# Putting the transfer queue of a top-k attention and feed-forward kernel into the program's order

## The chip, the core and the metric

The kernel runs on one core of a Trainium2 chip. Its engines are TensorE (PE, with weight loads shown apart as PEld), VectorE (DVE), ScalarE (ACT), GpSimd (POOL) and SyncE (SP). All transfers of this kernel are issued by SP, one after the other; "SPq" is that queue in the profile. The metric is the device time of one execution in microseconds, lower is better; shown is the median of the runs.

## What is computed

Inputs are q, k and v of 8 batches, 8 heads, 576 positions and 64 values per head, all float32, and two weight matrices of 512 x 2048 and 2048 x 512.

```python
scores = scale * np.matmul(q, k.transpose(0, 1, 3, 2))
kth = np.partition(scores, -top_k, axis=-1)[..., -top_k:-top_k + 1]      # top_k = 32
scores = np.where(scores >= kth, scores, -1000000000.0)
attn = np.exp(scores - np.max(scores, axis=-1, keepdims=True))
attn = attn / (np.sum(attn, axis=-1, keepdims=True) + 1e-09)
x = np.matmul(attn, v)            # then the heads side by side: (4608, 512)
h = x @ w_in
g = np.where(h >= 1, h, np.where(h <= -1, 0.0, (h + 1) ** 2 / 4.0))
out = g @ w_out
```

## The kernel before

**Steps.** A batch has four row tiles of 128 positions (t = 0 to 3) and a tail of 64 (t = 4). A step m treats two rows tiles of scores, 128 x 576 each: a pair of heads of a whole tile, or four heads of a tail. There are 144 steps; `steps` (line 606) lists them in rounds of two batches: b's four tiles (16 steps), b's tail (2), b+1's tail (2), b+1's four tiles (16).

**What a step does.** PE multiplies queries and keys (`sp`, L358), ACT copies the scores out (`s`, L359). DVE finds the 32nd largest of each row by repeated max and match-replace (L379 to L451) and masks the exponentials (L458); its reciprocal of the sums (`rz`, L404) opens the next step. POOL scales the weights `e` by it (L411). The weights are then needed with positions on partitions. In the first 8 steps and the last 2 PE transposes them (`transpose_w`). In the other 134 steps `move_w` (L484) does it through memory: ACT splits each 32-bit word into two 16-bit halves (`halves`, L488, one buffer), SP writes them out (`rows<-halves`, L490), waits until they have landed, and issues a transposing read (`wT<-rows`, L492; four `wT` buffers). PE multiplies `wT` by the values (`po`, L506, or L514 for tails), always for a pair of steps, in an even step: those of m-4 and m-3. The odd one of the pair is thus the one whose weights are fresher.

**Second layer.** Once all heads of 128 positions are there, `mlp` queues their matrix products (`ph`, L539, and `py`, L578). PE takes them in small portions spread over the following steps; the result `y` (L581) goes out at L583.

**Keys, queries and values of later batches.** From batch 2 on, keys and queries are turned in the same way as the weights. `turn` (L279) has ACT split a block into `parts` (L283, one buffer), writes `lines<-parts` (L285), and keeps the transposing read (`kT<-lines` or `qT<-lines`, L292) for `finish_turns`. `turned_keys_of` (L294) goes through five blocks of a batch's keys, one in every second step, each loaded by two or three transfers (`k_block`, L303 to L307) into one buffer. Its first call also starts `load_values` (L190): four loads of `v_in` (two buffers, so the batch before last must be done), two of `v_tail` for whole tiles and four for tails (L198, L203). `queries` (L706) turns the queries of a coming tile and fetches the next one's (`q_in`, L211, one buffer).

**Early part.** Before the second layer can start, its weights are converted in 32 pieces (`convert`, L632) in the first 8 steps; their words are loaded into `raw` and into the parts of `kT` and `v_in` that aren't used yet (L134). Later, every second step, half a piece is loaded again and inspected (L169).

**Order.** `tc.manual_schedule` (L680) fixes the order of PE, DVE, ACT and POOL to that of the program. SP isn't in that list: the order of its transfers was chosen by the scheduler, which moves a transfer to a place where its inputs and buffer are expected to be free. The program's main loop (L766) runs seven slots for each step; `move_w` is called in slot 3, and calls `finish_turns` itself.

Of the kernel before, what the change touches and what calls it, by code (L numbers as in the profile page):

```python
# [11 lines left out]
F32 = mybir.dt.float32  # L12
U16 = mybir.dt.uint16
# [13 lines left out]
def kernel(  # L27
# [10 lines left out]
    nc = tc.nc  # L38
    B, H, S, D = q.shape
    NTOK, DM = out.shape  # L40
    DFF = moe_w_in.shape[1]
    P = 128
# [3 lines left out]
    NHP = H // 2  # L46
# [34 lines left out]

    v_tails = []
    for i in range(2):
        v_tails.append([const.tile([P, H, D], F32, name=f"v_tail{i}{x}") for x in range(2)])
        for x in v_tails[i]:
            nc.gpsimd.memset(x, 0.0)

# [89 lines left out]
    def run(ctx, paired):  # L177
# [12 lines left out]
        def load_values(b):  # L190
            v_in = stage.tile([P, H, NT, D], F32, name="v_in")
            v_tl = v_tails[b % 2]
            yield v_in, v_tl
            for h in range(0, H, 2):
                nc.sync.dma_start(out=v_in[:, h:h + 2], in_=whole(v, b)[:, h:h + 2])
                yield
            for j in range(2):
                nc.sync.dma_start(out=v_tl[0][j * TL:(j + 1) * TL, j::2, :],  # L198
                                  in_=v[b, j::2, SM:S, :].rearrange("h p d -> p h d"))
            yield  # L200
            for hp in range(NHP):
                g = hp % 2
                nc.sync.dma_start(out=v_tl[1][g * TL:(g + 1) * TL, 2 * hp:2 * hp + 2, :],  # L203
                                  in_=v[b, 2 * hp:2 * hp + 2, SM:S, :].rearrange("h p d -> p h d"))
                if g:
                    yield

        def load_queries(b, t):
            if t < NT:
# [75 lines left out]
            nc.sync.dma_start(out=lines, in_=parts)  # L285
            turns.append(partial(nc.sync.dma_start_transpose, dst.bitcast(U16), lines.rearrange("p t k -> (p t) k")))

        turns = []

        def finish_turns():  # L290
            while turns:
                turns.pop(0)()  # L292

        def turned_keys_of(b):  # L294

            kT = stage.tile([P, NHP, S], F32, name="kT")
            got = dict(kT=kT)

            def load_block(c):
                x = stage.tile([P, H, D], F32, name="k_block", tag="k_in", bufs=1)  # L300
                ends = k[b, :, SM:S, :].rearrange("h p d -> p h d")
                if c < NT:
                    nc.sync.dma_start(out=x[:, 0::2, :], in_=whole(k, b)[:, 0::2, c, :])  # L303
                    nc.sync.dma_start(out=x[TL:P, 1::2, :], in_=whole(k, b)[0:P - TL, 1::2, c, :])
                else:
                    nc.sync.dma_start(out=x[0:TL, 0::2, :], in_=ends[:, 0::2, :])
                nc.sync.dma_start(out=x[0:TL, 1::2, :], in_=whole(k, b)[P - TL:P, 1::2, c - 1, :] if c else ends[:, 1::2, :])  # L307
                return x

            blocks = {0: load_block(0)}  # L310
            got["loads"] = load_values(b)
            got["v"], got["v_tl"] = next(got["loads"])
            yield got
            for c in range(NT + 1):
                n = P if c < NT else TL
                turn(blocks.pop(c)[0:n], kT[:, :, c * P:c * P + n])
                if c < NT:
                    blocks[c + 1] = load_block(c + 1)
                yield got

        def turned_queries_of(q_in, t):
# [162 lines left out]
        def move_w(st):  # L484
            st["wT"] = wT = late.tile([P, BLOCKS, P], F32, name="wT", bufs=4)
            halves = late.tile([P, 2, 2 * S], U16, name="halves")
            for i in range(2):
                nc.scalar.copy(halves[:, :, i * S:(i + 1) * S], st["e"][:, i, :].bitcast(U16).rearrange("p (k t) -> p t k", t=2))  # L488
            rows = dram.tile([P, 2, 2 * S], U16, name="rows")
            nc.sync.dma_start(out=rows, in_=halves)  # L490
            finish_turns()
            nc.sync.dma_start_transpose(wT.bitcast(U16), rows.rearrange("p t k -> (p t) k"))  # L492

        def block(i, c):
            return i * (NT + 1) + c if c < NT else NT
# [2 lines left out]
        def values(st):  # L498
            t, hp, v_in, v_tl = st["t"], st["hp"], st["keys"]["v"], st["keys"]["v_tl"]
            wT = st["wT"]  # L500
            po = ps.tile([P, P], F32, name="po", tag="ph", bufs=3)
            if t < NT:
                for c in range(NT + 1):
                    for j in range(2):
                        h = 2 * hp + j
                        nc.tensor.matmul(po[j * D:(j + 1) * D], v_in[:, h, c, :] if c < NT else v_tl[0][:, h, :],  # L506
                                         wT[:, block(j, c)], start=(c == 0), stop=(c == NT))
            else:
                for i in range(2):
                    cols = slice(i * TL, (i + 1) * TL)  # L510
                    for c in range(NT + 1):
                        for j in range(2):
                            h = 2 * (hp + i) + j
                            nc.tensor.matmul(po[j * D:(j + 1) * D, cols], v_in[:, h, c, :] if c < NT else v_tl[1][:, h, :],  # L514
                                             wT[:, block(i, c), part(i, j)],
                                             start=(c == 0), stop=(c == NT))
            xT, col = st["xT"]
            if t < NT:
                nc.scalar.copy(xT[:, hp, col:col + P], po)
            else:  # L520
                nc.scalar.copy(xT[:, hp:hp + 2, col:col + TL], po.rearrange("p (i n) -> p i n", i=2))
# [149 lines left out]
        def advance(amount, until):  # L671
# [4 lines left out]
            while pending and due >= pending[0][0] and pe_time < until and take():  # L676
# [1 line left out]
            due = min(due, 24.0)  # L678

        order = tc.manual_schedule(engines={mybir.EngineType.PE, mybir.EngineType.DVE, mybir.EngineType.Activation,  # L680
                                            mybir.EngineType.Pool})
        order.__enter__()
        keys, xTs = {}, {}
        q_ins, qTs = {}, {}
# [1 line left out]
        def fetch(i):  # L686
            if i < len(rounds) and rounds[i] not in q_ins:
                q_ins[rounds[i]] = load_queries(*rounds[i])
# [17 lines left out]
        def queries(m):  # L706
            nonlocal pe_time
            if m < n and steps[m][0:2] not in qTs:
                r = steps[m][0:2]
                if r[0] > 1:  # L710
                    qTs[r] = turned_queries_of(q_ins[r], r[1])
                else:
                    qTs[r] = queries_of(q_ins[r], r[1], nc.vector.tensor_copy if m == 0 else nc.scalar.copy)
                    pe_time += 0.5
                fetch(rounds.index(r) + 1)

        def begin(m):
            b, t, hp, ch, col = steps[m]
# [20 lines left out]
        for i in range(2, len(room) or 2):  # L739
            load(words, i)  # L740
        queries(0)
        convert(12.0)
        begin_at(0)
        convert(13.0)
# [21 lines left out]
        for m in range(n + 2):  # L766
# [22 lines left out]
            for slot in range(SLOTS):  # L789
                now = start + (dve_time - start) * (slot + 1) / SLOTS  # L790
                for _ in range(parts[slot]):
                    next(top_k, None)
                if m < n and converted < n_pieces:
                    if slot in now_converting:
                        convert(now)
                elif slot == 3 and late is not None:
                    if m % 2:
                        inspect()
                    elif paired:
                        load(late, inspected, 1, 2)  # L800
                if slot == 1 and 1 <= m <= n and state[m - 1]["by_tensor"]:
                    pe_time = max(pe_time, done[m - 1] + 2.0) + 1.0
                    transpose_w(state[m - 1])
# [1 line left out]
                if slot == 3 and 1 <= m <= n and state[m - 1] is not None and not state[m - 1]["by_tensor"]:  # L805
                    move_w(state[m - 1])
                    ready_at[m - 1] = done[m - 1] + 15.0
                if slot == 3:
                    finish_turns()
                if slot == 2 and m == n and paired:  # L810
                    judge(ps, att)
                if slot == 2 and (early or m == first_late or m >= n - 1):
                    values_until(m)
# [14 lines left out]
                if slot == (6 if early else 1):  # L828
                    queries(m + (3 if early else 5))
                    if (m < n and prep is None and next_keys < B and steps[m][0] == next_keys - 1 and steps[m][1] >= 1  # L830
                            and (next_keys > 1 or converted == n_pieces)):
                        prep = (turned_keys_of if next_keys > 1 else keys_of)(next_keys)
                    if prep is not None and (m % 2 == 0 or next_keys == 1):
                        got = next(prep, None)
                        pe_time += 0.5 if next_keys < 2 else 0.0
                        if got is None:
                            prep, next_keys = None, next_keys + 1
                        else:
                            keys[next_keys] = got
                            value_loads = got.get("loads", value_loads)  # L840
                    elif value_loads is not None:
                        next(value_loads, None)
                if paired and early and spent == 0 and not pending:
                    rest = ps.tile([P, NT, P], F32, name="rest", tag="py", bufs=1)
                    for i in range(5):
# [59 lines left out]
```

## Time and profile before

| | |
|---|---|
| time, median of 3 runs | 1481.04 us (1479.47 to 1487.06) |
| profiled execution | 1484.11 us |
| its span | 1482.2 us |
| busy: PE, DVE | 1435.8, 1403.9 us |
| busy: ACT, POOL | 1158.0, 926.6 us |
| DMA queue | 510144 packets, 258.80 MB, 66.4% of 16 engines |
| writes `rows<-halves` | 134, 576 KB each |
| transposing reads `wT<-rows` | 134, about 2.6 us of SP each, 4.7 us from issue to landing |
| loads `v_tail<-in_v_dram` | 16 of 64 KB and 32 of 32 KB |
| granted PE clock, mean | 0.992 |

Busy times are unions of the intervals in which an engine works; they come from the one profiled execution. A line of a timeline gives start and duration in us, engine, source line, operation, written tile and what it is made from, the count of merged instructions, and in brackets the idle time before it and what ended that. A line of waits gives the waiting engine and line, what released it, the total in us, the number of times, and the longest. A line of the chain of waits gives start, duration and the work on the chain that ended last. Where an instruction waited for several things, the release names the one that came last in the records, which may not be the one that counted.

### The profile page before, as it was taken

How to read it: one execution, taken by the hardware profiler on the slowest of the kernel's cores; microseconds unless marked ns; L12 is line 12 of the kernel's file. 1: busy time of each engine (PE TensorE's matmuls, PEld its weight loads, DVE VectorE, ACT ScalarE, POOL GpSimd, SP SyncE). 2: the span in 40 equal slices, each digit the busy share in tenths (PEclk: the TensorE clock that was granted, in tenths of full speed). 3: DMA queues.
4: the chain of work that ended last, by engine and by line, in shares of the span. 5: the costliest groups of instructions: out<-in, count | busy, mean ns of one | idle time of the engine just before them, and what ended most of it. 6: DMA issues, size and time to landing. Idle time of an engine off the chain costs nothing.

```text
span 1482.2 us, 32086 instructions
## 1 busy us (share of the span) xinstructions
PE 1435.8 (97%) x10755; PEld 1044.6 (70%) x10755; DVE 1403.9 (95%) x4392; ACT 1158.0 (78%) x2221; POOL 926.6 (63%) x1310
## 2 busy tenths in 40 slices
PE   6998899999999999999999999999999999999998
PEld 5766677777777777767777777677777777777675
DVE  6989999999999999999999999999999999999912
ACT  7987877878888887887778888788778888777632
POOL 3474566776676666566766677567666666666730
PEclk8999999999999999999999999999999999999999
DMA  8633657775677767787677787787677886665510
GB/s 252 196 121 107 177 152 203 196 194 162 167 206 204 193 193 205 193 209 174 163 195 203 196 198 194 195 214 183 174 197 187 202 202 167 168 166 142 149 25 17
DMA packets 510319, 260.94 MB, mean 176 GB/s; under 512 B 460992, under 2 KB 469184, under 8 KB 510144
## 3 DMA queue, kind: packets, MB, share of 16 engines
q1 hardware_dynamic: 510144, 258.80, 66.4%
q8 instruction: 87, 1.43, 0.4%
q14 instruction: 88, 0.72, 0.2%
HBM read 62.91 MB, written 102.63 MB: 112 GB/s over the span
## 4 chain that ended last, share of the span: by engine, by line
PE 80%; DVE 10%; DMA 4%; ACT 4%; issue 2%; SPq 1%; ACTq 0%; DVEq 0%
PE ph L539 30%; PE py L578 29%; PE sp L358 9%; PE po L506 9%; DVE more L379 2%; DMA rows<-halves 2%; DVE e L458 2%; DMA wT<-rows 1%; PE po L514 1%; DVE more L372 1%; DVE tops L420 1%; DVE tops L428 1%; DVE tops L392 1%; PE pw L473 1%; ACT halves L488 1%
## 5 line engine op out<-in xcount | busy, mean ns | idle before, releaser
L539 PEld LDWEIGHTS ph<-xT,w_in 128*128 128x128 f32 x4608 | 547.0, 192 | 102.6 <-issue 71.1
L539 PE MATMUL ph<-xT,w_in 128*128 128x128 f32 x4608 | 555.7, 276 | 2.3 <-ACT g L558 1.4
L578 PE MATMUL py<-w_out,g 128*128 128x512 f32 x1152 | 541.5, 597 | 1.8 <-ACT y L581 1.8
L565 POOL TENSOR_SCALAR r<-r 128x256 f32<-128x256 f32 x280 | 166.9, 596 | 413.4 <-ACT r L550 409.7
L379 DVE MATCH_REPLACE8 more<-tops,more 128x288 f32<-128x288 f32 x864 | 375.1, 437 | 0.0
L578 PEld LDWEIGHTS py<-w_out,g 128*128 128x128 f32 x1152 | 199.0, 191 | 166.5 <-issue 163.8
L488 ACT COPY halves<-e 128x1152 uint16<-128x1152 uint16 x268 | 293.6, 1143 | 18.5 <-DMA rows<-halves 18.1
L568 POOL TENSOR_TENSOR g<-r,g 128x256 f32<-128x256 f32 x280 | 241.6, 863 | 22.0
L458 DVE SCALAR_TENSOR_TENSOR e<-s,kth,e 128x577 f32<-128x577 f32 x288 | 246.9, 893 | 0.1
L411 POOL TENSOR_SCALAR e<-e,rz 128x576 f32<-128x576 f32 x268 | 235.9, 890 | 13.2 <-DVE rz L404 13.2
L395 ACT ACTIVATE e<-s,nmax 128x576 f32<-128x576 f32 x288 | 222.5, 773 | 4.7
L550 ACT ACTIVATE r<-ph,half 128x256 f32<-128x256 f32 (+1 forms) x296 | 136.1, 460 | 107.8 <-PE ph L539 99.7
L359 ACT ACTIVATE s<-sp 128x576 f32<-128x576 f32 x288 | 171.9, 649 | 61.7 <-PE sp L358 57.7
L567 POOL TENSOR_TENSOR r<-r 128x256 f32<-128x256 f32 x276 | 183.1, 663 | 23.0
L358 PE MATMUL sp<-kT,qT 64*128 64x288 f32 x1024 | 163.1, 436 | 8.3 <-ACT kT L261 6.1
L506 PE MATMUL po<-wT,v_in 128*64 128x128 f32 x2048 | 138.8, 277 | 8.0 <-DMA wT<-rows 4.6
L358 PEld LDWEIGHTS sp<-kT,qT 64*128 64x128 f32 x1024 | 90.0, 189 | 79.3 <-issue 37.2
L506 PEld LDWEIGHTS po<-wT,v_in 128*64 128x64 f32 x2048 | 113.6, 137 | 32.4 <-issue 10.3
L558 ACT ACTIVATE g<-ph,minus 128x256 f32<-128x256 f32 x280 | 130.4, 466 | 0.0
L372 DVE TENSOR_TENSOR more<-s 128x576 f32<-128x576 f32 x144 | 124.1, 862 | 6.0 <-ACT s L359 6.0
L420 DVE MAX8 tops<-more 128x8 f32<-128x288 f32 x288 | 125.4, 443 | 0.0
L372 DVE TENSOR_TENSOR less<-s 128x576 f32<-128x576 f32 x144 | 117.7, 817 | 0.0
(91 smaller groups left out, 1370.0 us busy)
## 6 DMA issues: line engine op xcount, KB each, us to landing
rows<-halves SPq DMA_DIRECT2D x134, 576.0 KB, 3.3
lines<-parts SPq DMA_DIRECT2D x48, 256.0 KB, 3.1
q_in<-in_q_dram SPq DMA_DIRECT2D x32, 256.0 KB, 3.8
v_in<-in_v_dram SPq DMA_DIRECT2D x32, 256.0 KB, 4.5
out_dram<-y SPq DMA_DIRECT2D x32, 256.0 KB, 3.9
raw<-in_moe_w_in_dram SPq DMA_DIRECT2D x32, 256.0 KB, 3.3
raw<-in_moe_w_out_dram SPq DMA_DIRECT2D x32, 256.0 KB, 3.5
kT<-in_moe_w_in_dram SPq DMA_DIRECT2D x8, 512.0 KB, 5.2
```

The source lines that it names most:

```text
L358: nc.tensor.matmul(*x, start=True, stop=True)
L372: nc.vector.tensor_tensor(out=x, in0=s[:, :, 0:SH], in1=s[:, :, SH:S], op=op)
L379: nc.vector.match_replace(out=st["rest"][:, i, :], in_to_replace=eight(st["tops"], i, r - 8), in_values=src[:, i, :], imm_value=LOWEST)
L395: nc.scalar.activation(e[:, i, :], s[:, i, :], AF.Exp, bias=nmax[:, i:i + 1])
L411: nc.gpsimd.tensor_scalar(st["e"][:, i, :], st["e"][:, i, :], rz[:, i:i + 1], 1.0, ALU.mult, ALU.mult)
L458: nc.vector.scalar_tensor_tensor(out=st["all"][1][:, i, :], in0=st["all"][0][:, i, :], scalar=last[i], in1=st["all"][1][:, i, :], op0=ALU. ...
L488: nc.scalar.copy(halves[:, :, i * S:(i + 1) * S], st["e"][:, i, :].bitcast(U16).rearrange("p (k t) -> p t k", t=2))
L506: nc.tensor.matmul(po[j * D:(j + 1) * D], v_in[:, h, c, :] if c < NT else v_tl[0][:, h, :], wT[:, block(j, c)], start=(c == 0), stop=(c == ...
L539: nc.tensor.matmul(ph[:, i], w_in[:, kk, f * P:(f + 1) * P], xT[:, kk], start=(kk == 0), stop=(kk == NK - 1))
L567: nc.gpsimd.tensor_tensor(out=r, in0=r, in1=r, op=ALU.mult)
L568: nc.gpsimd.tensor_tensor(out=g, in0=r, in1=g, op=ALU.add)
L578: nc.tensor.matmul(py[0], gs[f // group][:, f % group], w_out[:, f, :], start=(f == 0), stop=(f == NF - 1))
```

## The change

SP joins the engines that keep the program's order, and the program now says in which order its transfers go. `turns` still holds reads of lines; two more lists hold the reads of rows and the loads, and `issue` empties a list. A step issues the reads of rows of the step before in slot 0; lines where `turn` is called (slot 1); the load for inspection in slot 1 instead of slot 3; rows in slot 3, then the reads of lines, then the loads of keys, queries and values, which were only noted when they came up. In the last three steps and after, a read of rows may go in any slot.

The loads of tails get fewer: a tail step's values now come from two places. Heads whose half of the partitions is right in the first tile (`v_tl[0]`) are taken from there; the second tile (`v_tl[1]`) is half as large and holds the other four heads, with two transfers instead of four. The check of the inspection (`judge`) moves from slot 2 of step n to the end of step n+1.

```diff
-        v_tails.append([const.tile([P, H, D], F32, name=f"v_tail{i}{x}") for x in range(2)])
+        v_tails.append([const.tile([P, H // (x + 1), D], F32, name=f"v_tail{i}{x}") for x in range(2)])
...
             yield
-            for hp in range(NHP):
-                g = hp % 2
-                nc.sync.dma_start(out=v_tl[1][g * TL:(g + 1) * TL, 2 * hp:2 * hp + 2, :],
-                                  in_=v[b, 2 * hp:2 * hp + 2, SM:S, :].rearrange("h p d -> p h d"))
-                if g:
-                    yield
+            for x in range(2):
+                nc.sync.dma_start(out=v_tl[1][x * TL:(x + 1) * TL, x::2, :],
+                                  in_=v[b, x + 1::4, SM:S, :].rearrange("h p d -> p h d"))
+            yield
+
+        def tail_values(v_tl, h, t):
+
+            if t == NT and h % 2 != h // 2 % 2:
+                return v_tl[1][:, h // 4 * 2 + h // 2 % 2, :]
+            return v_tl[0][:, h, :]
...
-        turns = []
-
-        def finish_turns():
-            while turns:
-                turns.pop(0)()
+        turns, loads, reads_of_rows = [], [], []
+
+        def issue(x):
+            while x:
+                x.pop(0)()
...
-            blocks = {0: load_block(0)}
+            blocks = {}
+
+            def load_later(c):
+                loads.append(lambda: blocks.update({c: load_block(c)}))
+
+            load_later(0)
...
-                    blocks[c + 1] = load_block(c + 1)
+                    load_later(c + 1)
...
             nc.sync.dma_start(out=rows, in_=halves)
-            finish_turns()
-            nc.sync.dma_start_transpose(wT.bitcast(U16), rows.rearrange("p t k -> (p t) k"))
+            reads_of_rows.append(partial(nc.sync.dma_start_transpose, wT.bitcast(U16), rows.rearrange("p t k -> (p t) k")))
...
-                        nc.tensor.matmul(po[j * D:(j + 1) * D], v_in[:, h, c, :] if c < NT else v_tl[0][:, h, :],
+                        nc.tensor.matmul(po[j * D:(j + 1) * D], v_in[:, h, c, :] if c < NT else tail_values(v_tl, h, t),
...
         order = tc.manual_schedule(engines={mybir.EngineType.PE, mybir.EngineType.DVE, mybir.EngineType.Activation,
-                                            mybir.EngineType.Pool})
+                                            mybir.EngineType.Pool, mybir.EngineType.SP})
...
-                fetch(rounds.index(r) + 1)
+                loads.append(partial(fetch, rounds.index(r) + 1))
...
         queries(0)
+        issue(loads)
         convert(12.0)
...
+                if slot == 0 or m >= n - 3:
+                    issue(reads_of_rows)
...
                     if m % 2:
                         inspect()
-                    elif paired:
-                        load(late, inspected, 1, 2)
...
+                if slot == 1 and late is not None and paired and m % 2 == 0:
+                    load(late, inspected, 1, 2)
                 if slot == 3:
-                    finish_turns()
-                if slot == 2 and m == n and paired:
+                    issue(turns)
+                    issue(loads)
+                if slot == SLOTS - 1 and m == n + 1 and paired:
                     judge(ps, att)
...
                     elif value_loads is not None:
-                        next(value_loads, None)
+                        loads.append(partial(next, value_loads, None))
```

More of the change, by code (lines that the diff above doesn't have):

```diff
@@ L513, in values @@
                             h = 2 * (hp + i) + j
-                            nc.tensor.matmul(po[j * D:(j + 1) * D, cols], v_in[:, h, c, :] if c < NT else v_tl[1][:, h, :],
+                            nc.tensor.matmul(po[j * D:(j + 1) * D, cols], v_in[:, h, c, :] if c < NT else tail_values(v_tl, h, t),
                                              wT[:, block(i, c), part(i, j)],
```

## The prediction

> **What bounds the kernel now.** I read the busy shares first, then the windows of 60 us, the chain of waits, and the timelines of PE and of the transfer queue (SPq) where the chain leaves PE.
>
> ```profile
> PE 1435.8 (97%) x10755; PEld 1044.6 (70%) x10755; DVE 1403.9 (95%) x4392; ACT 1158.0 (78%) x2221; POOL 926.6 (63%) x1310
> ```
>
> Two engines are full. The windows (length, then busy us of PE, PEld, DVE, ACT, POOL, then clock, DMA share, GB/s) show where one isn't:
>
> ```profile
> 480.00:540.00 60.00, 60.00 (x494) 45.11 (x496) 60.00 (x193) 52.19 (x100) 38.43 (x55) 1.00 0.76 197
> 540.00:600.00 60.00, 58.66 (x516) 42.19 (x512) 60.00 (x192) 46.88 (x91) 42.00 (x59) 1.00 0.76 207
> 600.00:660.00 60.00, 56.67 (x391) 40.87 (x391) 60.00 (x182) 46.67 (x88) 34.82 (x51) 0.97 0.79 200
> 660.00:720.00 60.00, 60.00 (x444) 43.15 (x441) 60.00 (x190) 47.57 (x95) 43.74 (x60) 1.00 0.69 169
> 900.00:960.00 60.00, 58.05 (x480) 41.57 (x479) 60.00 (x190) 45.55 (x86) 37.63 (x54) 0.97 0.78 201
> ```
>
> DVE reads 60.00 in every window from 180 to 1380 us; PE reads 60.00 except where a batch's values end and the next keys are turned (240 to 300, 540 to 660, 900 to 1020). The chain prices those places on PE's own clock:
>
> ```profile
> 538.56 2.34 PE po L506 x40
> ...
> 576.30 2.48 PE po L514 x80
> ...
> 587.25 5.12 DMA rows<-halves
> ...
> 608.83 3.44 DMA rows<-halves
> ...
> 619.36 5.51 DMA rows<-halves
> 630.49 3.52 DMA rows<-halves
> ...
> 659.04 2.33 PE po L506 x40
> ...
> 1268.07 2.48 PE po L514 x80
> ...
> 1343.90 2.33 PE po L506 x40
> ```
>
> Four steps take 37.74 us (538.56 to 576.30), 9.44 a step. From the same place in a round, the eight steps 1268.07 to 1343.90 take 75.83, and 576.30 to 659.04 take 82.74: 6.9 lost. 923.30 to 1003.80 in the same chain is 80.50: 4.7 lost. 195.65 to 273.83 is 78.18 against 75.81 (1230.32 to 1306.13): 2.4; 273.83 to 312.04 another 0.5. Together 14.4 us. What the queue does in the first place:
>
> ```profile
> 585.55 1.61 SPq L195 DMA_DIRECT2D v_in<-in_v_dram  x3
> 587.25 0.41 SPq L490 DMA_DIRECT2D rows<-halves  x1
> 587.71 3.35 SPq L203 DMA_DIRECT2D v_tail<-in_v_dram  x4
> 592.43 2.34 SPq L492 DMA_TRANSPOSE wT<-rows  x1
> ```
>
> ACT ended these halves at 583.70; the write of rows went out at 587.25, behind key blocks, a key read and values. Its read went out at 592.43, and PE stood 1.34 us before `po` at 597.07. ACT has one `halves` tile, so its next copies waited for that write to land (1.09, 2.27 and 2.74 us at 612, 625 and 634), and the delay went from step to step to this:
>
> ```profile
> 638.66 1.21 PE L506 MATMUL po<-wT,v_in 128*64 128x128 f32 x16 [2.52 <-ACT parts L283]
> ```
>
> The release named is ACT, but the read of 634.03 plus the usual 4.7 us to land is 638.7: it is the transfer. The queue's idle time before its reads:
>
> ```profile
> SPq L492 <- DMA rows<-halves: 301.9, 117, 4.9
> ```
>
> **What the Trainium skill says.** DMA: Bandwidth & Descriptors, section "Anatomy of one DMA": DMA engines don't wait on semaphores, the issuing sequencer does, before dispatch. The trace agrees: the 301.9 us above are SPq's, 2.83 at best per read, and whatever stands behind waits too. The same page, "Two DMAs through the same engine are not ordered": a transfer that reads what another writes needs that one's completion; so the wait can be filled, not dropped. SBUF — State Buffer, "Who interferes with whom": a DVE instruction with two SBUF inputs excludes a GpSimd one that reads SBUF. The trace agrees: L458 takes 0.81 us with POOL idle at 1402 us, and 1.29 beside POOL here:
>
> ```profile
> 698.53 1.29 DVE L458 SCALAR_TENSOR_TENSOR e<-s,kth,e 128x577 f32<-128x577 f32 x1
> ```
>
> TensorE: Matmul & The Clock Gate, "What's actually happening": too little PE activity lowers its clock. The 2.52 us gap is followed by `sp` x8 in 2.29 us instead of 1.24, and 600 to 660 has 0.97.
>
> **The change, part by part.** In the built program PE, ACT, DVE and POOL keep their orders, but for one 0.27 us transpose (`pworst`) that goes behind one `po` group near the end: 0 us, since that group waits for the same ACT copies. So everything is on SPq.
>
> *Rows, reads, loads.* Before, a bunch of loads could stand before a write of rows. Now a step issues lines, rows, the key or query read, then its loads, and the rows' read opens the next step. At 583.70 the write would go at once: 3.5 us earlier; likewise by 5.4 us at 608.83 (halves ended 603.37) and 4.8 at 619.36 (614.55). Between write and read of a key-turning step now stand the key read (1.27) and three block loads (0.62 each): with the write's 0.36, 3.5 us, where the landing alone asks 2.83. The read itself goes 0.7 later after its write, but the write is 3.5 to 5.4 earlier. PE takes an odd step's weights 8.9 us after the read in the quiet rounds (706.94 to 715.84), 4.2 more than landing: 3.5 remain. All 14.4 us could go; I leave 1.0 for a read that still comes late.
>
> *Fewer tails.* 16 of 32 loads of 32 KB go, 0.60 us of queue each, in one place 3.35 to about 1.3. They are split over steps; this is within the sum above. Two fills of half size spare POOL 0.5 us at the start: hidden.
>
> *First values load.* It now stands in the odd step after turning begins, and waits for PE to finish the old batch: rows 574.11, PE done at 578.6, so SPq stands 4 us, the read behind it. That read serves an even step, needed at 594.34: no cost. The lines behind it go at about 582.6 instead of 577.17, with 583.70 for the rows still met.
>
> *Loads no longer hoisted.* Key pair 3 of batch 0 now follows a weight piece that DVE frees at 20.05: issue 20.5, landing near 25 instead of before 22.54 (PE's use). ACT copies it at 26.22 and DVE wants the scores at 32.83, 1.9 us after they are ready: bounds 0 and 2, I take 0. Key pair 3 of batch 1 goes from 138.45 to 140.09 + 2.83 + 2.6 + 0.5 = 146, landing 149 to 151 where PE asks at 148.94: 0 to 2 us, covered by the 3.34 us that PE waits at 159.71 anyway; 0. Values of batch 1 now move just before the write of 151.91; slower landing adds 0 to 2 to that 3.34; I take 0.
>
> *What is late next.* DVE. Its reciprocal of step 52 (the 53rd) stands at 545.59 and PE's `po` of that step at 576.23, 30.6 us later; after the stalls the distance is 38.1 (step 60), then it shrinks as DVE takes 9.5 to 9.7 a step, and stands still at 34.1 from step 104 to 136 and at 30.7 from 44 to 52, in both with DVE at 9.44. So DVE gives up the distance the stalls make; without stalls it should stay near 30.7. The end hangs on DVE (last reciprocal 1411.64, then 70.6 us of values and second layer), so from PE's gain go 34.1 - 30.7 = 3.4.
>
> Sum: 14.4 - 1.0 - 3.4 = 10.0 us. The profiled execution took 1484.11 (span 1482.2, 1.9 around it): 1474.1, which is 0.68% less; on the median 1481.04 that is **1471**.
>
> **The rivals.** *DVE keeps its own pace.* It shows no idle time in those windows, so PE's stalls may never have reached it. Then time stays: 1481, or 1478 if half passes. For it: 60.00 throughout. Against it: DVE's 9.44 wherever PE isn't disturbed for long.
> *Half of the stalls stay:* landings of rows under load take 5.1 us instead of 2.83, and odd reads keep their lateness. 7.2 - 1.7 = 5.5 gained: 1475.5.
> *Slower: the read behind the turn.* Six batches have five turning steps each; in these 30 places the odd step's read now stands behind a key read that itself waits for its lines. If lines land late (their ACT copy is about 6 us ahead of the rows, landing 3.1), the read comes over 7.0 us after its write instead of 3.5, and PE's 4.2 are gone. That is the point from which it decides. At 0.5 us in each of 30 places the 15 outweigh what is won elsewhere (5): 1491. Against it: lines at 597.01, rows ready 603.37.
> *It doesn't do what it says:* the order is in the program, so no chance.
>
> **How the numbers follow.** Under 0.5% (7.4 us) a measurement can't tell this kernel from no change. Chances: forecast 0.57 (1466 to 1475), half of the stalls or DVE's pace 0.31 (1475 to 1484), slower 0.12 (1485 to 1495). Range: from all 14.4 us and a little of the start gained (1465) to the upper end of no change, 1484. Part of the forecast's upper edge counts as no change: faster 0.56, same 0.31, slower 0.13.
>
> **What would show it.** Right: rows written within 0.1 us of their halves in the turning steps; no ACT wait on rows; eight steps from 576 to 659 in 76 to 77 us and PE clock 1.00 in 600 to 660; the distance staying at 31. Wrong: reads more than 7 us after writes and PE waits on `wT` in turning steps; DVE at 9.5 a step with PE waiting for weights; a longer first 180 us.

## The result and the profile after

| | before | after |
|---|---|---|
| time, median (17 runs each) | 1482.07 us (1479.46 to 1487.06) | 1476.62 us (1473.67 to 1479.75) |
| ratio | | 0.9962, 95% interval 0.9952 to 0.9971 |
| profiled execution, its span | 1484.11, 1482.2 us | 1475.20, 1473.3 us |

The change takes 0.38% off: the sign of the forecast and about half of its size on the median. The interval leaves no room for no change at all, although the prediction held anything under 0.5% to be too little to tell. In a second round of executions, the last of the experiments, the ratio was 0.9990. The busy line of the page after, to be held against that of before (PE 1435.8, DVE 1403.9):

```profile
PE 1435.0 (97%) x10755; PEld 1045.2 (71%) x10755; DVE 1395.3 (95%) x4392; ACT 1159.3 (79%) x2221; POOL 925.3 (63%) x1310
```

PE does the same work. VectorE does the same instructions in 8.6 us less, so its instructions themselves got shorter; the part on what paces the steps comes back to that. The windows where PE stood before (length, busy us of PE, PEld, DVE, ACT, POOL, clock, DMA share, GB/s):

```profile
540.00:600.00 60.00, 60.00 (x525) 43.48 (x520) 60.00 (x192) 48.32 (x93) 42.12 (x60) 1.00 0.73 189
600.00:660.00 60.00, 59.80 (x428) 43.29 (x427) 60.00 (x192) 51.10 (x96) 40.38 (x57) 1.00 0.91 221
...
900.00:960.00 60.00, 60.00 (x526) 44.31 (x523) 60.00 (x192) 50.96 (x98) 38.99 (x56) 1.00 0.86 214
```

PE had 58.66, 56.67 and 58.05 there, and a clock of 0.97 in two of them; it has 60.00, 59.80 and 60.00, and 1.00. The queue in a step that turns keys (start, duration, what it issues), ACT having ended the halves at 583.48:

```profile
583.51 0.34 SPq L499 DMA_DIRECT2D rows<-halves  x1
586.11 1.25 SPq L296 DMA_TRANSPOSE kT<-lines  x1
587.40 0.58 SPq L307 DMA_DIRECT2D k_block<-in_k_dram  x1
...
589.42 3.39 SPq L296 DMA_TRANSPOSE wT<-rows  x1
```

The write goes 0.03 us after its halves, where such writes went 3.5 to 5.4 us late. Counted over the 134 writes in the two traces, 39 went out more than 1 us after their halves before, 5.5 us at most; now 4 do, 1.4 at most. ACT's waits for rows ahead of its copies of halves fell from 18.1 us to 0.3. The read of this step, though, comes 5.9 us after its write instead of the 3.5 reckoned, since the key read ahead of it waits 2.3 us for its lines. Over the whole run the queue's idle time, by what ended it:

```profile
SPq L296 <- DMA rows<-halves: 170.4, 87, 3.4
...
SPq L296 <- DMA lines<-parts: 48.3, 38, 2.6
```

301.9 us of waiting for rows became 170.4, but not all of that is filled with other transfers: the same reads also wait for PE, and with those waits they hold the queue for 411.8 us in all, where it was 483.9. Against that stand 48.3 us of waiting for lines, 15.9 before.

PE's own clock says where the time went. This table is worked out from PE's timelines: us between the first `po` matmul of one step and that of another, and the absolute start for steps 12 and 136. The lowest value in a column comes nearest to what PE itself needs there. The names are those of the experiments below; the run with less work for PE is left out.

| kernel | step 12 at | 12 to 20 | 20 to 24 | 24 to 52 | 52 to 60 | 60 to 88 | 88 to 96 | 96 to 124 | step 136 at | span |
|---|---|---|---|---|---|---|---|---|---|---|
| before | 195.58 | 78.17 | 38.21 | 264.27 | 82.73 | 264.27 | 80.50 | 264.27 | 1381.61 | 1482.22 |
| before, second execution | 195.43 | 78.65 | 38.21 | 264.27 | 79.09 | 264.27 | 80.02 | 264.27 | 1377.81 | 1478.84 |
| tails_only | 196.17 | 78.63 | 38.63 | 264.27 | 77.70 | 265.20 | 77.94 | 264.27 | 1376.43 | 1478.88 |
| order_only | 198.97 | 81.43 | 38.21 | 264.27 | 82.14 | 264.27 | 80.74 | 265.01 | 1388.66 | 1489.95 |
| loads_first | 196.29 | 78.86 | 38.21 | 264.27 | 82.50 | 264.27 | 79.86 | 264.27 | 1382.14 | 1482.75 |
| values_behind | 198.58 | 76.73 | 38.24 | 265.65 | 75.84 | 264.27 | 75.84 | 264.27 | 1373.03 | 1476.71 |
| reads_first | 199.26 | 77.42 | 39.32 | 273.03 | 83.69 | 272.13 | 85.33 | 272.76 | 1416.55 | 1516.50 |
| turns_last | 196.34 | 76.71 | 38.21 | 264.27 | 75.95 | 264.27 | 75.84 | 264.27 | 1369.46 | 1471.88 |
| start_early | 198.12 | 77.12 | 38.21 | 264.47 | 76.10 | 264.71 | 75.84 | 264.27 | 1372.45 | 1476.46 |
| dve_less | 196.34 | 77.45 | 38.21 | 264.27 | 75.84 | 264.27 | 75.84 | 264.27 | 1370.10 | 1470.61 |
| old_tails | 196.15 | 77.03 | 38.21 | 264.27 | 76.23 | 264.27 | 75.84 | 264.27 | 1369.87 | 1472.62 |
| after | 196.06 | 77.48 | 38.21 | 264.27 | 76.27 | 264.97 | 75.84 | 264.27 | 1370.97 | 1473.32 |
| after, second execution | 198.97 | 77.67 | 38.21 | 264.27 | 76.03 | 264.27 | 75.84 | 264.27 | 1373.14 | 1476.65 |

Outside the places where batches meet, PE takes the same 264.27 us in nearly all of these kernels, to a hundredth.

### The profile page after: what moved, and what is told of

Its sections match the earlier page's. It is cut to its first block, busy times and chain, and to the rows that moved or that the text cites. A ratio compares the mean times of both kernels' runs of the same rounds, so it can differ in the third digit from the quotient of the medians.

```text
span 1473.3 us, 32005 instructions
## 1 busy us (share of the span) xinstructions
PE 1435.0 (97%) x10755; PEld 1045.2 (71%) x10755; DVE 1395.3 (95%) x4392; ACT 1159.3 (79%) x2221; POOL 925.3 (63%) x1310
## 4 chain that ended last, share of the span: by engine, by line
PE 73%; DVE 19%; ACT 3%; issue 2%; DMA 2%; SPq 0%; ACTq 0%; DVEq 0%
PE ph L547 28%; PE py L586 27%; PE sp L367 9%; PE po L514 8%; DVE more L388 5%; DVE e L467 3%; DVE more L381 2%; DVE tops L429 2%; DVE tops L437 2%; DVE tops L448 1%; DVE seconds L455 1%; DVE less L381 1%; DVE tops L401 1%; PE pw L482 1%; PE po L522 1%
## 5 line engine op out<-in xcount | busy, mean ns | idle before, releaser
L573 POOL TENSOR_SCALAR r<-r 128x256 f32<-128x256 f32 x280 | 137.6, 492 | 406.1 <-ACT r L558 402.6
L420 POOL TENSOR_SCALAR e<-e,rz 128x576 f32<-128x576 f32 x268 | 303.6, 1143 | 11.9 <-DVE rz L413 11.9
L576 POOL TENSOR_TENSOR g<-r,g 128x256 f32<-128x256 f32 x280 | 231.8, 828 | 22.0
L467 DVE SCALAR_TENSOR_TENSOR e<-s,kth,e 128x577 f32<-128x577 f32 x288 | 240.4, 870 | 0.1
L381 DVE TENSOR_TENSOR more<-s 128x576 f32<-128x576 f32 x144 | 133.5, 927 | 7.3 <-ACT s L368 7.3
L429 DVE MAX8 tops<-more 128x8 f32<-128x288 f32 x288 | 125.3, 442 | 0.0
L401 DVE MAX8 tops<-more 128x8 f32<-128x288 f32 x288 | 116.2, 442 | 0.0
```

The lines of the kernel that those rows point to most:

```text
L381: nc.vector.tensor_tensor(out=x, in0=s[:, :, 0:SH], in1=s[:, :, SH:S], op=op)
L420: nc.gpsimd.tensor_scalar(st["e"][:, i, :], st["e"][:, i, :], rz[:, i:i + 1], 1.0, ALU.mult, ALU.mult)
L467: nc.vector.scalar_tensor_tensor(out=st["all"][1][:, i, :], in0=st["all"][0][:, i, :], scalar=last[i], in1=st["all"][1][:, i, :], op0=ALU. ...
L576: nc.gpsimd.tensor_tensor(out=g, in0=r, in1=g, op=ALU.add)
```

## The experiments

**The kernel before, once more** (before_again). No edit; one execution.

> The kernel before, unchanged, in another execution. The theory (PE loses time where rows go out behind loads; how much differs from one execution to the next, since VectorE's pace depends on when GpSimd's work meets it): the same three places lose time (after steps 12, 52 and 88), but the sum is not the 14.4 us of the profiled execution; with a time near 1482 the loss is 10 to 13 us. Rival (the loss is fixed by the order of the queue alone): the same 14.4 us within 0.5, whatever the time.

Measured: 1480.64 us. The three places lost 2.8 + 0.5 + 3.3 + 4.2 = 10.8 us by the prediction's own way of counting (78.65, 38.21, 79.09 and 80.02 against 75.81, 37.74, 75.83 and 75.83), not 14.4. The difference of 3.6 is almost the 3.47 us between the two executions. The order is the same, and the rows are nearly as late (22.4 us in the sum over steps 48 to 59, against 24.8), yet the eight steps after 52 lose half as much: the loss is not fixed by the order alone.

**The order alone** (order_only).

```diff
-                                            mybir.EngineType.Pool})
+                                            mybir.EngineType.Pool, mybir.EngineType.SP})
```

> The kernel before with the transfer queue put into its own program order, nothing else: loads and lines stand ahead of rows, the read of rows directly behind its write, the queue idle while rows land. Theory (what counts is that rows aren't kept behind loads that wait): loads come at the place where they are called, two slots ahead of the rows, so rows go out within 0.5 us of their halves in most steps; most of the gain is there, 1476 to 1479. Rival (the gain comes from the reads put in the next step, work for the queue in place of idle time): queue blocked 2.8 us at each of 134 reads, 1482 or slower.

Measured: 1493.35 us, ratio 1.0078 (1.0065 to 1.0092). The expectation from the theory failed; a fixed order by itself costs. But not by the rival's reason either: between steps 24 and 52 the queue idles at each read and PE still takes 264.27. Step 136 comes 10.9 us later than in the second execution of the kernel before: 3.5 are lost ahead of step 12, 2.8 at 12 to 20, 3.1 at 52 to 60, and 0.7 each at 88 to 96 and 96 to 124. In the three places where batches meet, the first load of values stands in front of rows (the queue waits 24.4 us in 3 places for PE to end the old batch).

**Loads ahead of rows, in the changed kernel** (loads_first).

```diff
+                if slot == 3:
+                    issue(loads)
                 if slot == 3 and 1 <= m <= n and state[m - 1] is not None and not state[m - 1]["by_tensor"]:
                     move_w(state[m - 1])
...
                     issue(turns)
-                    issue(loads)
```

> The changed kernel with one thing undone: a step's loads go ahead of its rows instead of behind the rows and the reads of lines. Theory (rows behind loads were the loss): rows go out 1 to 2.5 us after their halves where key blocks or values are loaded and up to 4 us where values wait for PE to finish the old batch; time 1478 to 1482, the gain mostly gone. Rival (the gain came from the fixed order and the later reads, not from the place of the loads): 1476 to 1477, as the changed kernel.

Measured: 1484.82 us, ratio 1.0019 (1.0012 to 1.0026). The gain is gone, and the time lies above the 1482 expected at most. The queue's timeline after step 52 shows which load it is:

```profile
571.57 0.47 SPq L215 DMA_DIRECT2D q_in<-in_q_dram  x1
580.11 0.39 SPq L195 DMA_DIRECT2D v_in<-in_v_dram  x1
580.60 0.41 SPq L499 DMA_DIRECT2D rows<-halves  x1
```

After 572.04 the queue does nothing for 8 us: the load of values waits until PE has done with the buffer's old batch, and the rows stand behind it, 5.5 us after their halves, rows that PE itself will need.

**The same, but values stay behind the rows** (values_behind).

```diff
-                        loads.append(partial(next, value_loads, None))
+                        value_reads.append(partial(next, value_loads, None))
...
                     issue(turns)
+                    issue(value_reads)
```

> As the run with the loads ahead of the rows, but the loads of values stay behind them; only key blocks and queries go ahead. Theory (what costs there is the first load of values, for which the queue stands 24.3 us in 3 places until PE has done with the old batch, the rows of a step behind it): the eight steps after step 52 in 76 to 78 us, time 1476 to 1479. Rival (any load ahead of the rows costs): 1482 to 1485, as with all loads ahead.

Measured: 1475.69 us, ratio 0.9973 (0.9966 to 0.9980); the eight steps after 52 take 75.84 instead of 82.50. Key blocks and queries ahead of rows cost nothing that shows in the median; the waiting load of values costs it all. The short loads hardly delay the rows: the writes go out 17.9 us late in the sum over the run, against 57.6 with all loads ahead; the queue stands some 300 us of the run waiting for halves anyway. Of the place of loads against rows, this is the part that counts.

**Reads of rows directly behind their writes** (reads_first).

```diff
-                if slot == 0 or m >= n - 3:
-                    issue(reads_of_rows)
...
                     move_w(state[m - 1])
+                    issue(reads_of_rows)
```

> The changed kernel with the read of rows directly behind its write, ahead of the step's reads of lines and loads; the queue idles 2.8 us while the rows land. Theory (reads that come 5 to 7 us after their rows cost PE only some 2 us in all, at the odd steps 19, 59 and 80 to 85): reads 2.8 to 3.2 us after rows everywhere, no PE wait on wT in turning steps, time 1474.5 to 1476.5, a gain of 0 to 2 us over the changed kernel's 1476.6. Rival (an idle queue is dear: loads and lines come late, as where the order alone was fixed): 1480 or slower.

Measured: 1518.16 us, ratio 1.0250 (1.0236 to 1.0264), as the rival said, and far beyond its 1480. Two views show why, the queue first, then ACT:

```profile
475.50 0.38 SPq L499 DMA_DIRECT2D rows<-halves  x1
480.07 2.44 SPq L296 DMA_TRANSPOSE wT<-rows  x1
...
483.91 1.55 SPq L307 DMA_DIRECT2D k_block<-in_k_dram  x1
```

```profile
488.83 1.04 ACT L287 COPY parts<-k_block 128x1024 uint16<-128x1024 uint16 x1 [3.68 <-DMA k_block<-in_k_dram]
```

The load of the next key block goes 8.4 us after the rows instead of 3.0 (470.19 to 473.15 in the changed kernel). ACT wants that block at 485.15 and stands 3.68 us; behind it in ACT's order are the copies of scores for both PE and VectorE. Over the run ACT waits 39.8 us for key blocks in 14 places, and PE loses in every stretch where keys are turned (273.03 for 264.27). With the order alone the queue idled at each read too, but loads were issued ahead of the rows, and there 24 to 52 took 264.27. So the read in the next step is worth far more for the loads that it lets pass than for the read.

**Reads of lines behind the loads** (turns_last).

```diff
-                    issue(turns)
                     issue(loads)
+                    issue(turns)
```

> The changed kernel with a step's loads ahead of its reads of lines, so that the loads fill the time in which the queue waits for lines to land (48.3 us over 38 places). Theory (PE loses some 2 us in all by reads of rows that stand behind those waits): reads of rows some 1 us earlier in key-turning steps, 1475 to 1476.6. Rival (the first load of values, which waits for PE, now holds the reads of lines too): 1477 to 1479.

Measured: 1476.15 us, ratio 0.9976 (0.9969 to 0.9982), as the theory has it. 12 to 20 falls from 77.48 to 76.71 and 52 to 60 from 76.27 to 75.95: about 1 us for the reads that came late, in one execution each.

**The tails, one way and the other** (tails_only and old_tails). The kernel before with only the fewer loads, and the changed kernel with the four loads that were there before. Shown is the second, without the tile sizes and matmuls that go with it; the first is its reverse:

```diff
-            for x in range(2):
-                nc.sync.dma_start(out=v_tl[1][x * TL:(x + 1) * TL, x::2, :],
-                                  in_=v[b, x + 1::4, SM:S, :].rearrange("h p d -> p h d"))
-            yield
+            for hp in range(NHP):
+                g = hp % 2
+                nc.sync.dma_start(out=v_tl[1][g * TL:(g + 1) * TL, 2 * hp:2 * hp + 2, :],
+                                  in_=v[b, 2 * hp:2 * hp + 2, SM:S, :].rearrange("h p d -> p h d"))
+                if g:
+                    yield
```

> The kernel before with the fewer loads of tails alone, the order still left to the scheduler. 16 transfers of 0.60 us of queue less, in bunches of 4 that become 2. Theory (order is the change, tails are little): 1481 to 1482, no more than 1.5 us of gain. Rival (the bunch of tail loads ahead of rows was the trouble): 1477 to 1479.

> The changed kernel with the 32 tail loads of 32 KB as before, in the new order. Theory (two loads of tails fewer in a step are 1.2 us of queue in 8 steps, behind rows and with room ahead of the read): 1476 to 1477.5, no difference that counts. Rival (the tails hold a read of rows up, as the prediction had it within the sum): 1478 to 1480.

Measured: 1480.80 us, ratio 0.9999 (0.9988 to 1.0010), for the first; 1476.46 us, 0.9977 (0.9968 to 0.9985), for the second. No difference that can be measured in either direction, though in the one profiled execution of tails_only the two later places lose 2 us each instead of 3 to 7. Rows are as late there as before (44 writes by more than 1 us).

**The start** (start_early). The last key pair of batch 0 is loaded with the one before it, the values of batch 1 ahead of its turning, and until step 13 reads of rows stand behind the loads of keys:

```diff
+                if b == 0 and hp < 2:
+                    ahead.append(load_keys(hp + 1))
+                    if hp == 1:
+                        ahead.append(load_keys(hp + 2))
...
+            if b:
+                value_loads_of(b, got)
             yield got
...
-                if slot == 0 or m >= n - 3:
+                if slot == (0 if m > 13 else 2) or m >= n - 3:
```

> The changed kernel with the early loads put ahead again: the last key pair of batch 0 together with the one before, the values of batch 1 ahead of its turning, and until step 13 the read of rows behind the loads of keys. It is the cost that the prediction took as 0. Theory (in the profiles the start up to step 12 differs by 0.5 us): 1475.5 to 1476.6, so 0 to 1 us gained. Rival (the new PE waits of 2.6 and 2.2 us at the start are lost time): 1472 to 1473.

Measured: 1477.32 us, ratio 0.9969 (0.9960 to 0.9978): no gain. The edit doesn't decide the question: PE's waits for keys are gone, but the later read makes PE stand 3.42 us for weights at 162, so step 12 comes at 198.12, no earlier. A cleaner one was not run.

**What paces the steps** (dve_less and pe_less). First less of VectorE, then less of PE:

```diff
-            for i in range(2):
-                replace(st, 24, i)
+            replace(st, 24, 0)
```

> The changed kernel with less work on VectorE: of the two match-replaces ahead of the last search of a step one is left out (one list of rows gets wrong thresholds; the flag for a second pass is held at zero). 0.51 us of VectorE less in each of 144 steps. Theory (PE paces the steps at 9.44 us; VectorE is kept busy to the full by waiting for the port beside GpSimd): time 1470 to 1475, VectorE now with idle time or with longer two-input instructions. Rival (VectorE at 60.00 of 60 is the bound): 144 x 0.51 = 73 us less, 1404.

```diff
-                for c in range(NT + 1):
+                for c in (range(NT + 1) if st["by_tensor"] else (0, 2, 3, 4)):
```

> The changed kernel with less work on PE: of the ten matmuls of a whole-tile step's values two are left out (one of four blocks of positions isn't summed). 0.117 us of PE less in 118 of the steps, 13.8 us in all. Theory (PE paces): steps of 9.32 in place of 9.44, VectorE follows since it needs 9.15 where GpSimd doesn't meet it, 1462 to 1465. Rival (VectorE paces at its own 9.44): 1475 to 1477.

Measured: 1474.37 us (ratio 0.9952, 0.9939 to 0.9966) and 1463.48 us (0.9885, 0.9865 to 0.9906). Against the changed kernel's 0.9962 and 1476.62 us, the work taken from VectorE is worth 1.5 us by the ratios and 2.3 by the medians, 13.8 us of PE's are worth 11.4 and 13.1. What VectorE was spared is less than the 73 us expected: a match-replace and the load of its values take 0.44 and 0.07 us, but overlap, and the next instruction starts 0.42 us after the first of the two, some 60 us in 144 steps. PE paces, in a kernel whose VectorE reads 60.00 of 60 in every window from 180 to 1380 us. How both can be is in the instruction groups (busy us, mean ns, then idle before), of the changed kernel:

```profile
L467 DVE SCALAR_TENSOR_TENSOR e<-s,kth,e 128x577 f32<-128x577 f32 x288 | 240.4, 870 | 0.1
```

and of the kernel with less VectorE work:

```profile
L388 DVE MATCH_REPLACE8 more<-tops,more 128x288 f32<-128x288 f32 x720 | 313.6, 437 | 0.0
L466 DVE SCALAR_TENSOR_TENSOR e<-s,kth,e 128x577 f32<-128x577 f32 x288 | 282.0, 1014 | 0.6 <-ACT e L404 0.5
```

The match-replaces fall by 61 us, and the same 288 masking instructions take 41.6 us more. Sorted by whether they overlap an instruction of GpSimd, in the changed kernel the 166 that overlap none all take 800 to 820 ns, and the other 122 take 953 in the mean and 1817 at most. With less VectorE work 262 of the 288 overlap one, with a mean of 1035. So VectorE runs ahead until its two-input instructions meet GpSimd's, and waits inside them; such a wait is counted as busy. That PE sets GpSimd's timing is argued, not tested. The meeting agrees with the Trainium skill, SBUF — State Buffer, "Who interferes with whom": a VectorE instruction with two inputs in SBUF contends with a GpSimd instruction that reads SBUF, and the lock on the port pair that the two share is exclusive.

**The changed kernel, once more** (after_again).

> The changed kernel unchanged, in other executions on this chip. Theory (without the stalls an execution has little to vary in, PE paces it): 1474 to 1479, median within 1 us of 1476.6, ratio to before 0.9955 to 0.9970. Rival (the gain was luck of the phase): a ratio over 0.998.

Measured: 1478.14 us against 1479.89 for the kernel before in the same round, ratio 0.9990 (0.9981 to 0.9999). The sign stays, the size doesn't, and the number is the rival's, over 0.998. Luck of the phase isn't shown by it, though: its table row shows all the places mended as before, and step 12 at 198.97 instead of 196.06.

## Why the prediction was right or wrong

*Where the time goes: right.* Rows stood late behind loads, and the loss left with the lateness: the three places gave 6.5, 4.7 and 0.7 us between the two profiled executions. That loads ahead of the rows can take the whole gain is shown by putting them back; how much of it the later reads have isn't separated. The eight steps after 52 take 76.27 us, within the 76 to 77 named, and the clock of 600 to 660 is 1.00. In a fixed order one load is dear, the first of a batch's values. The prediction saw its wait (4 us put down; 4.5 at most measured, 8.7 in 3 places) and rightly priced it at nothing behind the rows; with rows behind it, it costs the whole gain. In the kernel before this load hardly waits (1.7 us for PE in all); there a bunch of loads stood ahead of the rows, and which of its members cost what isn't separated: the fewer tails alone changed nothing.

*"All 14.4 us could go": the term that was too large.* 14.4 was the loss of one execution, 3 us above the median, and it was taken off the median. In the second execution of the same kernel it is 10.8. Against its own execution the sum came out near: 1474.1 forecast, 1475.20 measured. That is in part luck: 13.4 were to be won by step 136 and 10.6 were, 3.4 were to be given back after it and 1.7 were, two errors that cancel in part. Carried over to the median it gave 1471, where 1476.62 was measured. That number lies nearer to the 1475.5 of "half of the stalls stay", but not for its reason: of the stalls, 1.9 us or less are left. Two parts of the 14.4 were never there to be had: the 0.5 at 20 to 24, where every kernel of the table takes 38.21 or more, and 0.9 of the 2.4 at 12 to 20, where the best takes 76.71 against the 75.81 it was held to.

*1.0 left for reads still late: somewhat low.* Against the best kernels the changed one loses 0.8 at 12 to 20, 0.4 at 52 to 60 and 0.7 at 60 to 88 in one execution, 1.9 in all, and 1.0, 0.2 and nothing in the other.

*3.4 given back with VectorE's distance: too much.* The distance, at every fourth step, did stay between 30.5 and 31.3 us from step 36 to 136. But PE's 10.6 us at step 136 became 8.9 at the end, 1.7 given back; between the two second executions 4.7 became 2.2, 2.5 given back. That VectorE only follows is shown by the run with less of its work, so "keeps its own pace" falls as the cause.

*Loads no longer hoisted, "I take 0": near in one execution, too little in the other.* PE stood for both key loads (2.56 and 2.22 us) in the first:

```profile
24.89 1.09 PE L261 MATMUL pk<-ident,xT 128*128 128x128 f32 x4 [2.56 <-DMA xT<-in_k_dram]
...
151.60 1.09 PE L261 MATMUL pk<-ident,k_in 128*128 128x128 f32 x4 [2.22 <-DMA k_in<-in_k_dram]
```

and in the second execution of the changed kernel for the first of them:

```profile
25.54 1.09 PE L261 MATMUL pk<-ident,xT 128*128 128x128 f32 x4 [3.14 <-DMA xT<-in_k_dram]
```

In the three profiles with the scheduler's order, which have no wait for these keys, step 12 begins at 195.43 to 196.17. In the first execution of the changed kernel it begins at 196.06, so both waits together cost next to nothing there; in the second it begins at 198.97. The other profiles of the table with the queue in program order and a wait for these keys fall into the same two groups. Where the first key wait is 2.4 to 2.7 us (five, the first execution among them) step 12 comes at 196.06 to 196.34; where it is 2.96 to 3.44 (four) at 198.58 to 199.26. The run with less work for PE lies between, 2.56 and 197.65. So the cost is about nothing or about 3 us; that the longer wait makes the difference isn't shown, since the one edit against it (step 12 at 198.12) moved a read as well.

*The slower rival.* It needed reads more than 7.0 us after their rows; they came up to 6.3 after them in the odd key-turning steps, once 7.2 in an even one, and cost 1 to 2 us at most, by the losses left above. The opposite danger, a queue that waits for each row and lets loads come late, wasn't among the rivals, and is the dear one: 41.5 us more than the changed kernel.

*Open:* why the gain is 1.8 us in the second round and 5.4 in the first; the kernel before was 2.2 us faster in the second. The start explains 2.9 us between the two executions of the changed kernel, but a profile shows one execution, and how often which start occurs wasn't measured. values_behind and turns_last are at 0.9973 and 0.9976 in the round where the changed kernel is at 0.9990; the first's interval ends just below the changed kernel's, the second's just reaches it. Their medians are 2.4 and 2.0 us lower; the places of the table explain about 1 us.

## What to carry to other kernels

On a queue that issues in order, look for the transfer that waits for the engine that will later want what stands behind it: with the order fixed, one load of values that waited for PE cost the whole gain, while key blocks and queries in the same place, which hardly delayed the rows, cost nothing that was measured. Fill a landing time with other transfers rather than idling in it, and check whose loads fall late if you don't. And count a loss in two executions before you take it off a median.

## What the runs showed of the hardware that was not expected

An engine can read as fully busy and not be the bound: with 0.42 us of work per step taken away VectorE stayed at 60.00 of 60 in three windows between 480 and 1140 us, its masking instructions growing from 870 to 1014 ns in the mean, all of it in those that overlap GpSimd's. The distance between VectorE and PE settles at a few values at which VectorE's pace equals PE's 9.44 us a step: 30.6 us in the changed kernel, 30.6 and later 34.1 in the one before, 35.1 with less VectorE work.
